# Fused attention, MLP and gate: the last 96 MLP features as extra columns of two projection units, exponentials kept in PSUM, and the additions of the products with V on GpSimd

## The chip, the cores and the metric

The kernel runs on one core of a Trainium2 chip. The metric is device time in microseconds (us), the median of several executions. In the text PE is TensorE, DVE is VectorE, ACT is ScalarE, POOL is GpSimd and SP is SyncE, which issues the DMAs.

## The reference

`x` is 2048 tokens of 512 numbers in fp32. Cut to what matters:

```python
xn = layernorm(x)
# A: sliding, dilated attention: 32 heads of 16, each token sees 8 tokens, 2 apart
q, k, v = split(xn @ wqkv)                     # 512 -> 3 * 512
logits = einsum("hsd,hswd->hsw", q, k[pos - 2*w]) * 16**-0.5   # w = 0..7, -1e9 where pos-2w < 0
s = einsum("hsw,hswd->hsd", softmax(logits), v[pos - 2*w]) @ wo
# B: MLP, F = 1376 features, and the gate
h = gelu(layernorm(xn) @ w1 + b1)              # 512 -> 1376 = 10 * 128 + 96
g = silu(h @ w2 + b2)                          # 1376 -> 512
out = x + s * g
```

## The kernel before

**Matmuls.** Every fp32 operand of a large matmul is written as a sum of two fp16 numbers (hi and lo), and three of the four cross products are computed, so 512 input features take 4 x 3 = 12 matmuls of 128x128 weights. Three kinds of work fill PE:

- *Projection units.* Tokens 0, 2, 4, ... and 1, 3, 5, ... are two residue classes `c`; with 4 blocks of 8 heads (`hb`) they give 8 units `u`. `qkv(c, hb, u)` computes one unit: 8 token tiles `i`, each 12 matmuls with 384 moving columns (128 each of q, k, v) into one PSUM tile, which ACT copies into `U[u % 2]` (L825). DMAs then copy the rows that neighbouring partitions need.
- *MLP.* The tokens are 4 chunks `ch` of 512; the 1376 features are 11 tiles `f`, the last of 96 (`FL`). `mlp1` (L1112) computes one feature tile of a chunk in 12 matmuls of 512 columns into a PSUM tile `mh`; ACT applies GELU there (L1129) and writes the fp16 hi part (L1133); DVE writes the lo part (L1137). For three early tiles PE subtracts hi in PSUM by a diagonal matrix `dg` instead (L1143) and ACT writes lo (L1146). `mlp2` (L1159) then takes the tile, two tiles later (`LAG`), in 4 x 3 matmuls of 512 columns into four accumulating PSUM tiles `z`. The 96-feature tile has its own buffer `hlast`, with a row of ones for the bias of the second layer, written by POOL (L1312).
- *Output projection.* L1026, from the transposed attention outputs `oT`.

**Attention of a unit** is elementwise, on DVE: 4 products q·k of 128x2048 (L873) each followed by a reduction (L877) into the logits `L` (128x512 in SBUF); maximum and subtraction (L908, L909); the exponential on ACT, in place (L912); sum, reciprocal and normalisation (L914 to L916); then 4 products with V, `pv(0)` to `pv(3)`, 128x2048 each (L946; L998 for the last unit), which have to be added up: 2048 + 2048 + 2048 down to 1024 numbers. DVE does some of these additions (L937). The rest, 128x1024 each, are put on POOL (L978) beside the next unit's reductions: `beside` puts a one-element copy from the next unit's product ahead of each (`gate`, L977), so that the addition starts once that product is done and runs while DVE reduces it. Then `emit_o` writes the output as hi (ACT, L925) and lo (DVE, L927), and a transposing DMA brings it into `oT`.

**Order.** `Plan` collects all operations with estimated durations, dependencies and priorities, and places them in the order of one simulated execution (with drawn disturbances, `SEEDS`). Each engine then runs its queue in that fixed order. Rings of buffers (`Ring`) are shared out in the same order. The PSUM has eight banks of 128x512 fp32: rings `ps` (2) and `mh` (2), and four `z`.

Of the kernel before, what the change touches and what calls it, by code (L numbers as in the profile page):

```python
# [19 lines left out]
P = 128  # L20
# [4 lines left out]
FL = F - (NF - 1) * P  # L25
NI = 8
# [8 lines left out]
W1C = [0, 2048, 4096, 5120, KT * F]  # L35
# [60 lines left out]
class Plan:  # L96
# [238 lines left out]
    def issue(self):  # L335
# [4 lines left out]
        for t, o in order:  # L340
# [4 lines left out]
SEEDS = ((500165, 389854, 427978, 647943, 394648, 289068, 629827, 866434, 58414, 290909, 969430, 478841,  # L345
          326988, 34468, 300308, 816254, 306888, 41293, 60788, 308971, 890734, 237800, 376148, 36800, 231455,
          772755, 355690, 761464),)
# [17 lines left out]
PS1 = 0.72  # L365

# [26 lines left out]
def tile_mixer(ctx, tc, a_x, a_wqkv, a_wo, b_w1, b_b1, b_w2, out):  # L393
# [47 lines left out]
    wq = sb.tile([P, NHB, 2, KT, 384], F16, name="wq")  # L441
    w1 = sb.tile([P, 2, KT, F], F16, name="w1")
# [7 lines left out]
    hlast = sb.tile([P, 2, 512], F16, name="hlast")  # L450
# [12 lines left out]
    R_ps = Ring(psum, [P, 512], F32, 2, "ps")  # L463
    R_mh = Ring(psum, [P, 512], F32, 2, "mh")
# [109 lines left out]
    def prep_q(hb):  # L574
        col = R_s.new()
        for k in range(0, KT, 2):
            def go(k=k):
                src = stq[hb]()[:, k * 384:(k + 2) * 384]
                nc.scalar.activation(wq[:, hb, 0, k:k + 2].bitcast(BF16),
                                     src.rearrange("p (k e) -> p k e", k=2), AF.Square,  # L580
                                     accum_out=col.t[:, k // 2:k // 2 + 1])
            act(768, go, [("stq", hb, k)] + ([("yf", 2)] if hb == 0 and k else []), [(col, k), ("wqh", hb, k), ("wqh", hb, k + 1)],
                aps=2, holds=stkey[hb])
# [194 lines left out]
    IORD, IORD0 = [2, 3, 1, 4, 5, 6, 7, 0], [2, 3, 0, 1, 4, 5, 6, 7]  # L778

    def qkv(c, hb, u):  # L780
# [13 lines left out]
        for n, i in enumerate(IORD if u else IORD0):  # L794
# [3 lines left out]
            b = (R_mh if more else R_ps).new()  # L798

            def mm(n0=0, n1=12, y=y, o=o, b=b):  # L800
                for n in range(n0, n1):
                    (s, t), k = ((0, 0), (1, 0), (0, 1))[n // KT], n % KT
                    nc.tensor.matmul(b.t[:, 0:384], y[:, s, k, o:o + P], wq[:, hb, t, k],  # L803
# [11 lines left out]
            for n0, n1 in zip([0] + ends, ends):  # L815
                pe(n1 - n0, 384, lambda mm=mm, n0=n0, n1=n1: mm(n0, n1), [("yh" if n1 <= 4 else "y", c, i)] +
                   [("wq" if n1 == 12 else "wqh", hb, k) for k in range(min(n1, KT))], [b],
                   after=pl.users([b]) | (left if n0 == 0 else set()), slack=QSLACK if u > 1 and n0 == 0 else 0.0)
            rw = [b, csk[i], ("kz", ub)], [("q", ub, i), ("k", ub, i), ("v", ub, i)]
            if i in on_dve:  # L820
# [6 lines left out]
                AF.Identity, scale=cs.t[:, cp(i):cp(i) + 1]), *rw, prio=PEV)  # L827

# [29 lines left out]
    def attention(c, hb, u):  # L858
# [9 lines left out]
        for n, g in enumerate(range(4)):  # L868
# [34 lines left out]
        def over_r(t):  # L903
# [8 lines left out]
        act(512, lambda: nc.scalar.activation(L.t, L.t, AF.Exp, scale=DH ** -0.5), Lk + [("warm",)], Lk, aps=0,  # L912
            table="exp", prio=PEV, hold=False)
        dve(512, lambda: nc.vector.tensor_reduce(sx.t, Lt(), AX.X, ALU.add), Lk, [sx], port=False)  # L914
        dve(64, lambda: nc.vector.reciprocal(sx.t, sx.t), [sx], [sx], f=6.0, port=False)
        dve(512, lambda: nc.vector.tensor_tensor(Lt(), Lt(), over_r(sx.t), op=ALU.mult),  # L916
            [sx] + Lk, Lk)
# [21 lines left out]
        if u < 7:  # L939
# [5 lines left out]
            def pv_to(g, dst, w):  # L945
                dve(2048, lambda: nc.vector.tensor_tensor(  # L946
                    dst().rearrange("p (r f d) -> p r f d", r=2, d=DH),
                    L3()[:, 2 * g:2 * g + 2].rearrange("p r (f o) -> p r f o", o=1)
                    .to_broadcast([P, 2, 64, DH]),
                    slots(Ut, VH, 2 * g).rearrange("p r (f d) -> p r f d", d=DH), op=ALU.mult),  # L950
                    Lk + vk + [("vh", ub, 0), ("vh", ub, 1), ("vh0", ub)], w)

            def addto(a, b):
                add(2048, lambda: a.t, lambda: b.t, lambda: a.t, [a, b], a)
            acc = pv(0)
            p1 = pv(1)
            if u in OWN:

                t2 = f32v(oT, 1)[:, 0, 2048:4096]
                pv_to(2, lambda: t2, [("p2",), ("oTst", 2)])  # L960
                addto(acc, p1)
                p3 = pv(3)
                add(1024, lambda: acc.t[:, 0:1024], lambda: t2[:, 0:1024], lambda: acc.t[:, 0:1024], [acc, ("p2",)], acc)
            else:
                p2 = pv(2)
                addto(acc, p1)
                p3 = pv(3)
                addto(acc, p2)
# [4 lines left out]
            def beside(x, y, upper=False):  # L973
                def go(pr, p=PR_U * (u + 1) + 500):
                    def fn():
                        d = x.t[:, 1024:2048] if upper else x.t[:, 0:1024]
                        nc.gpsimd.tensor_copy(gate, pr.t[0:1, 0:1])  # L977
                        nc.gpsimd.tensor_tensor(d, d, y(), op=ALU.add)  # L978
                    pool(2.45, fn, [acc, p3, pr] + [("p2",)] * (u in OWN), [x, ("gate",)], prio=p)
                return go  # L980
# [4 lines left out]
            if u in OWN:  # L985
                pend.append(beside(acc, lambda: t2[:, 1024:2048], True))
            pend.extend([beside(acc, lambda: acc.t[:, 1024:2048]),
                         beside(p3, lambda: p3.t[:, 1024:2048]),
                         beside(acc, lambda: p3.t[:, 0:1024]), rest])
        else:  # L990

            for h in range(2):
                m = []
                for g in range(2):
# [53 lines left out]
    def wo_last():  # L1048
        rings = [R_ps, R_ps, R_mh, R_mh] + R_z
# [50 lines left out]
    def w1_parts(k, f0, f1):  # L1100
        return [m for m in range(4) if W1C[m] < k * F + f1 and W1C[m + 1] > k * F + f0]

    def mlp1(ch, f):
        M = P if f < NF - 1 else FL
# [4 lines left out]
        def mm(n0, n1):  # L1109
            for n in range(n0, n1):  # L1110
                k, (s, t) = n // 3, ((0, 0), (0, 1), (1, 0))[n % 3]
                nc.tensor.matmul(b.t[0:M], w1[:, s, k, f * P:f * P + M], yT[ch][:, t, k],  # L1112
                                 start=(n == 0), stop=(n == 11))

        for n0 in range(0, 12, 3) if ch == 0 and f < 3 else (0,):
# [3 lines left out]
               [("w1", m) for k in range(n0 // 3, n1 // 3) for m in w1_parts(k, f * P, f * P + M)], [b],  # L1119
               after=pl.users([b]))  # L1120
        if f < NF - 1:
            h = R_h.new()
            hi, lo = (lambda: h.t[:, 0]), (lambda: h.t[:, 1])
        else:
            h = ("hlast",)
            hi, lo = (lambda: hlast[:, 0]), (lambda: hlast[:, 1])
        hk = (h, 0) if f < NF - 1 else ("hlast", 0)
        with prio(PR_H + pl.prio * 1e-6):
            act(512, lambda: nc.scalar.activation(  # L1129
                b.t[0:M], b.t[0:M], AF.Gelu_apprx_tanh, bias=b1T[0:M, f:f + 1],  # L1130
                scale=hsc[0:M, 1:2]), [b, ("b1T",), ("hsc",)], [b], aps=2, table="gelu")

            act(512, lambda: nc.scalar.activation(hi()[0:M], b.t[0:M], AF.Identity,  # L1133
                                                  scale=hsc[0:M, 2:3]),
                [b] + [("hseq", NF * ch + f - 1)] * (NF * ch + f > 0), [hk, ("hseq", NF * ch + f)])
            if NF * ch + f in DVE_LO:
                dve(512, lambda: nc.vector.scalar_tensor_tensor(  # L1137
                    lo()[0:M], b.t[0:M], hsc[0:M, 2:3], hi()[0:M], op0=ALU.mult,
                    op1=ALU.subtract), [b, hk], [h], port=False, c=0.14)
                hq[f] = (hi, lo, M if f < NF - 1 else M + 1, h, hk)  # L1140
                return

# [323 lines left out]
```

## Time and profile before

| what | value |
|---|---|
| three executions | 412.53, 413.24, 413.51 us; median 413.24 |
| span of the profiled execution | 411.5 us (the time of an execution is some 1.8 us more: 413.24 - 411.5) |
| PE busy | 406.5 us, 99% of the span, 2086 matmuls |
| DVE busy | 387.3 us, 94%, 372 instructions |
| ACT busy | 222.4 us, 54% |
| POOL busy | 114.8 us, 28% |
| DMA | 44.83 MB, mean 109 GB/s |

The profile holds one execution. Instructions of a line, operation and shape form a group with a count, a busy time and the mean of one in ns; busy times of matmuls include their pipelined ends, so the distance from one matmul's start to the next one's is read from the chain that ended last. Idle time in front of an instruction is put down to the engine or the DMA that released it.

### The profile page before, as it was taken

To read this page: it belongs to the slowest core of one execution; us is meant where nothing else is said; L and a number is where in the kernel's file an instruction comes from. 1 tells how busy PE (TensorE), PEld (TensorE's weight loads), DVE (VectorE), ACT (ScalarE), POOL (GpSimd) and SP (SyncE) were. 2 spreads that over 40 slices of the span, in tenths; PEclk is the share of its full clock that TensorE was granted. 3 is DMA by queue.
4 is the path that set the end of the run, shared out by engine and by line. 5 is a ranking of instruction groups with operands and counts; after the bars stand their busy time and mean duration, and the time that the engine had idled before them with its cause. 6 is when DMAs were issued, how large, how long until landed. Compare 5 with 4: busy or idle time off the path is not lost.

```text
span 411.5 us, 5549 instructions
## 1 busy us (share of the span) xinstructions
PE 406.5 (99%) x2086; PEld 206.7 (50%) x2086; DVE 387.3 (94%) x372; ACT 222.4 (54%) x357; POOL 114.8 (28%) x160
## 2 busy tenths in 40 slices
PE   8999999999999999999999999999999999999996
PEld 5565544446544554455444644445655554444443
DVE  4999999999999999999999989999989999999955
ACT  4999999976479377332673261127311582244500
POOL 6620442052822150015201500055037400340022
PEclk9999999999999999999999999999999999999999
DMA  8972350500343557600740070302063356008034
GB/s 289 414 268 86 89 205 2 204 2 1 91 99 132 63 159 170 83 0 2 178 165 2 0 165 29 104 0 74 4 205 115 102 181 165 0 2 256 2 78 177
DMA packets 42666, 44.83 MB, mean 109 GB/s; under 512 B 27496, under 2 KB 27936, under 8 KB 42128
## 3 DMA queue, kind: packets, MB, share of 16 engines
q1 hardware_dynamic: 42640, 44.49, 36.8%
q8 instruction: 16, 0.26, 0.3%
q14 instruction: 10, 0.08, 0.1%
HBM read 23.53 MB, written 7.34 MB: 75 GB/s over the span
## 4 chain that ended last, share of the span: by engine, by line
PE 97%; DMA 1%; DVE 1%; SPq 0%; POOL 0%; issue 0%
PE z L1159 28%; PE ps L803 27%; PE mh L1112 26%; PE ps L1026 6%; PE mh L803 2%; PE z L1026 2%; PE mh L1026 1%; PE ps L1112 1%; DMA prod<-in_A_x_dram 1%; PE z L705 1%; PE mh L810 1%; DVE U L1082 0%; DVE U L1085 0%; DVE bn L662 0%; PE ps L810 0%; POOL lw L636 0%
## 5 line engine op out<-in xcount | busy, mean ns | idle before, releaser
L1112 PE MATMUL mh<-yT,w 128*128 128x512 f16 (+1 forms) x504 | 115.7, 379 | 0.0
L803 PE MATMUL ps<-wq,yT 128*128 128x384 f16 x684 | 115.0, 326 | 0.0
L1159 PE MATMUL z<-w,h 128*128 128x512 f16 x480 | 110.8, 379 | 0.0
L803 PEld LDWEIGHTS <-yT 128*128 128x128 f16 x744 | 72.3, 98 | 49.4 <-ACT yT L720 0.4
L1112 PEld LDWEIGHTS <-w 128*128 128x128 f16 (+1 forms) x528 | 52.8, 100 | 60.9
L1129 ACT ACTIVATE mh<-mh,b1T,hsc 128x512 f32<-128x512 f32 (+1 forms) x42 | 31.5, 750 | 87.1 <-PE mh L1112 87.0
L1159 PEld LDWEIGHTS <-h 128*128 128x128 f16 x480 | 46.8, 98 | 55.6
L873 DVE TENSOR_TENSOR prod<-U 128x2048 f32<-128x2048 f32 x32 | 72.9, 2282 | 1.3 <-DMA U<-U 0.9
L877 DVE TENSOR_REDUCE L<-prod 128x128 f32<-128x2048 f32 x32 | 73.1, 2285 | 0.8
L825 ACT ACTIVATE U<-ps,cs 128x384 f32<-128x384 f32 x56 | 32.4, 579 | 60.6 <-PE ps L803 59.1
L946 DVE TENSOR_TENSOR prod<-L,U 128x2048 f32<-128x2048 f32 x25 | 60.0, 2422 | 0.2
L977 POOL COPY gate<-prod 1x1 f32<-1x1 f32 x24 | 4.2, 175 | 156.6 <-DVE prod L873 156.6
L978 POOL TENSOR_TENSOR prod<-prod 128x1024 f32<-128x1024 f32 x14 | 32.8, 2346 | 0.0
L1026 PEld LDWEIGHTS <-oT 128*128 128x128 f16 x204 | 19.8, 98 | 21.7
L937 DVE TENSOR_TENSOR prod<-prod,prod 128x2048 f32<-128x2048 f32 x13 | 29.7, 2282 | 0.0
L1026 PE MATMUL ps<-wo,oT 128*128 128x512 f16 (+1 forms) x132 | 28.5, 367 | 0.0
L1133 ACT ACTIVATE h<-mh,hsc 128x512 f16<-128x512 f32 x38 | 26.0, 684 | 0.8
L1137 DVE SCALAR_TENSOR_TENSOR h<-mh,hsc,h 128x512 f16<-128x512 f32 x36 | 26.3, 731 | 0.1
L978 POOL TENSOR_TENSOR prod<-prod,oT 128x1024 f32<-128x1024 f32 x3 | 10.0, 3324 | 41.6 <-DVE prod L937 41.6
L1019 POOL TENSOR_TENSOR f<-f,f 128x512 f32<-128x512 f32 x4 | 10.6, 2655 | 21.9 <-DMA U<-U 18.2
L978 POOL TENSOR_TENSOR prod<-prod,prod 128x1024 f32<-128x1024 f32 x7 | 16.4, 2346 | 0.0
L1019 POOL TENSOR_TENSOR U<-U,f 128x512 f32<-128x512 f32 x4 | 5.5, 1380 | 34.9 <-DVE U L1091 34.9
(184 smaller groups left out, 406.4 us busy)
## 6 DMA issues: line engine op xcount, KB each, us to landing
f<-in_A_x_dram SPq DMA_DIRECT2D x31, 256.0 KB, 3.6
U<-U SPq DMA_DIRECT2D x16, 392.0 KB, 3.9
gd<-f SPq DMA_DIRECT2D x12, 256.0 KB, 3.5
oT<-in_B_w_dram SPq DMA_DIRECT2D x2, 1024.0 KB, 9.5
yT<-in_B_w_dram SPq DMA_DIRECT2D x2, 1024.0 KB
f<-gd SPq DMA_DIRECT2D x8, 256.0 KB, 3.4
out_dram<-f SPq DMA_DIRECT2D x8, 256.0 KB, 3.0
out_dram<-U SPq DMA_DIRECT2D x7, 256.0 KB, 2.0
```

What stands on the lines that cost most here:

```text
L803: nc.tensor.matmul(b.t[:, 0:384], y[:, s, k, o:o + P], wq[:, hb, t, k], start=(n == 0), stop=(n == 11))
L825: act(384, lambda i=i, b=b: nc.scalar.activation(U3[:, i:i + 31:15, :], b.t[:, 0:384].rearrange("p (t e) -> p t e", t=3), AF.Identity, sca ...
L873: first = dve(2048, lambda p2=p2, g=g: nc.vector.tensor_tensor(p2(), q, slots(Ut, KH, 2 * g), op=ALU.mult), qk + [("kh", ub, 0), ("kh", ub ...
L877: first.then = dve(2048, lambda pr=pr, g=g: nc.vector.tensor_reduce(L3()[:, 2 * g:2 * g + 2], pr.t.rearrange("p (r f d) -> p r f d", r=2, ...
L937: dve(n, lambda: nc.vector.tensor_tensor(d(), a(), b(), op=ALU.add), keys, [dkey])
L946: dve(2048, lambda: nc.vector.tensor_tensor(dst().rearrange("p (r f d) -> p r f d", r=2, d=DH), L3()[:, 2 * g:2 * g + 2].rearrange("p r (f ...
L978: nc.gpsimd.tensor_tensor(d, d, y(), op=ALU.add)
L1026: nc.tensor.matmul(b.t[:, cols], oT[:, hb, i // 4, s, i % 4], wo[:, t, hb, cols], start=(hb == 0 and n == 0), stop=(hb == last and n == 2))
L1112: nc.tensor.matmul(b.t[0:M], w1[:, s, k, f * P:f * P + M], yT[ch][:, t, k], start=(n == 0), stop=(n == 11))
L1129: act(512, lambda: nc.scalar.activation(b.t[0:M], b.t[0:M], AF.Gelu_apprx_tanh, bias=b1T[0:M, f:f + 1], scale=hsc[0:M, 1:2]), [b, ("b1T",) ...
L1137: dve(512, lambda: nc.vector.scalar_tensor_tensor(lo()[0:M], b.t[0:M], hsc[0:M, 2:3], hi()[0:M], op0=ALU.mult, op1=ALU.subtract), [b, hk], ...
L1159: nc.tensor.matmul(z.t, hl[s][0:K, t * P:(t + 1) * P], w2[0:K, w, f], start=(f == 0 and n == 0), stop=(f == NF - 1 and n == 2))
```

## The change

1. **The last 96 features in two projection units.** The units `u = 2` and `u = 6` (head block 2 of each residue class) get weights `wqr` of 384 + 96 columns: the last 96 columns of `w1` stand beside those of q, k and v. Their 16 token tiles take 480 moving columns a matmul. The `mlp1` of the 96-feature tile and `hlast` go. Since these features now come out with tokens on partitions, a new chain `rest1` handles a chunk: ACT copies 4 times 96 columns out of PSUM, POOL adds the bias, ACT does GELU and hi over 128x384, DVE lo, POOL writes the column of ones, and one transposing DMA writes `hlT`, from which `mlp2` of `f = 10` reads.
2. **No subtraction on PE.** The three L1143 matmuls, `dg` and the ACT lo parts go; DVE writes all lo parts.
3. **Exponentials in PSUM.** ACT writes the exponentials to a PSUM tile `E`, and the sum, the normalisation and the products with V read it there. `ps` and `mh` become one ring of 3 banks; `E` has 1.
4. **Additions on POOL.** For `u < 7` POOL does all additions of the products with V as seven of 128x1024: two right behind `pv(1)`, without a gate, and five gated, four on the next unit's products and one on its shifted logits. For the last unit POOL does the first addition of the first half. `emit_o` comes one step later than before.
5. The seeds of the plan differ, and with them, and with the new operations, the order on all engines. `PREST` sets when the last piece of the `w1` split is placed. One more small DMA loads the bias of the 96 features (`b1r`).

```diff
-    w1 = sb.tile([P, 2, KT, F], F16, name="w1")
+    wqr = sb.tile([P, 2, KT, 384 + FL], F16, name="wqr")
+    wqs = sb.tile([P, NHB - 1, 2, KT, 384], F16, name="wqs")
+    w1 = sb.tile([P, 2, KT, FM], F16, name="w1")
...
-    R_ps = Ring(psum, [P, 512], F32, 2, "ps")
-    R_mh = Ring(psum, [P, 512], F32, 2, "mh")
+    R_ps = R_mh = Ring(psum, [P, 512], F32, 3, "ps")
+    R_E = Ring(psum, [P, 512], F32, 1, "E")
...
+        rest = u in RESTU
+        ncol = 384 + FL * rest
...
-                    nc.tensor.matmul(b.t[:, 0:384], y[:, s, k, o:o + P], wq[:, hb, t, k],
+                    nc.tensor.matmul(b.t[:, 0:ncol], y[:, s, k, o:o + P], wqr[:, t, k] if rest else wq[hb][:, t, k],
...
+            if rest:
+                ch = 2 * c + i // 4
+                hp = hrest[ch] = hrest.get(ch) or R_f.new()
+                act(FL, lambda i=i, b=b, hp=hp: nc.scalar.activation(
+                    hp.t[:, i % 4 * FL:(i % 4 + 1) * FL], b.t[:, 384:384 + FL], AF.Identity, scale=hsc[:, 1:2]),
+                    [b, ("hsc",)], [(hp, i % 4)], prio=PEV)
...
-            if pend and (n or u - 1 in OWN):
-                pend.pop(0)(pr)
-                if n == 3:
-                    pend.pop(0)()
+            if pend:
+                pend.pop(0)(pr, [pr])
...
-        act(512, lambda: nc.scalar.activation(L.t, L.t, AF.Exp, scale=DH ** -0.5), ...
+        act(512, lambda: nc.scalar.activation(E.t, L.t, AF.Exp, scale=DH ** -0.5), ...
+        if pend:
+            pend.pop(0)(L, Lk)
+            pend.pop(0)()
...
-                    L3()[:, 2 * g:2 * g + 2].rearrange("p r (f o) -> p r f o", o=1)
+                    E3()[:, 2 * g:2 * g + 2].rearrange("p r (f o) -> p r f o", o=1)
...
+            def sums(x, s, y, keys):
+                pool(2.4, lambda: nc.gpsimd.tensor_tensor(x.t[:, s], x.t[:, s], y(), op=ALU.add), [x] + keys, [x])
...
-                addto(acc, p1)
-                p3 = pv(3)
-                addto(acc, p2)
+            for s in (lower, upper):
+                sums(acc, s, lambda s=s: p1.t[:, s], [p1])
...
+            pend.extend([beside(acc, upper, lambda: t2[:, upper], [pk]),
+                         beside(acc, lower, lambda: t2[:, lower], [pk]),
+                         beside(p3, lower, lambda: p3.t[:, upper], []),
+                         beside(acc, lower, lambda: acc.t[:, upper], []),
+                         beside(acc, lower, lambda: p3.t[:, lower], [p3]), rest])
...
+    def rest1(ch):
+        hp, h16 = hrest.pop(ch), R_f.new()
...
+        pool(..., lambda: nc.gpsimd.tensor_tensor(t3(), t3(), b1r..., op=ALU.add), ...)
+        pool(0.4, lambda: nc.gpsimd.memset(h4()[:, :, :, FL:P], 0.0), hk, [(h16, 2)], port=False)
+        pool(0.25, lambda: nc.gpsimd.tensor_scalar(h4()[:, :, 0, FL:FL + 1], ...
+        act(4 * FL, lambda: nc.scalar.activation(hp.t[:, 0:4 * FL], hp.t[:, 0:4 * FL], AF.Gelu_apprx_tanh),
+            hk, hk, aps=0, table="gelu")
+        act(4 * FL, lambda: nc.scalar.activation(h4()[:, :, 0, 0:FL], t3(), AF.Identity, scale=hsc[:, 2:3]), ...
+        dve(4 * FL, lambda: nc.vector.scalar_tensor_tensor(
+            h4()[:, :, 1, 0:FL], t3(), hsc[:, 2:3], h4()[:, :, 0, 0:FL], op0=ALU.mult, op1=ALU.subtract), ...
+        dma(P * 2048, lambda: nc.sync.dma_start_transpose(
+            hlT.rearrange("p t a k -> p (t a) k"), h16.t.bitcast(F16)), ...
...
-            pe(1, 512, lambda: nc.tensor.matmul(b.t[0:M], dg[0:M, 0:M], hi()[0:M], start=False,
-                                                stop=True, skip_group_check=True), ...
-            act(512, lambda: nc.scalar.activation(lo()[0:M], b.t[0:M], AF.Identity, ...
```

In the changed kernel's line numbers the projection stands on L807, `mlp1` on L1153 and `mlp2` on L1185; q·k product and reduction are L883 and L887, the products with V L960, the sum, reciprocal and normalisation of the exponentials L928 to L930, the lo parts of the MLP L1173 and of the outputs L941; the ungated additions are L970, the gate and the gated additions L987 and L988; `rest1` runs from L1122 to L1136.

Two places show how the queues differ. The first is DVE where the MLP starts, from the last pieces of the weight splits (L551, L552) to the lo parts of the first three feature tiles (`h` with three buffer numbers). In the kernel before:

```order
L551 SCALAR_TENSOR_TENSOR w_77<-h_104,hsc,w_77 128x384
L877 TENSOR_REDUCE L_101<-prod_91 128x2x64
L551 SCALAR_TENSOR_TENSOR w_78<-yT_82,zsc,w_78 128x1024 x2
L1137 SCALAR_TENSOR_TENSOR h_105<-mh_159,hsc,h_105 128x512
L877 TENSOR_REDUCE L_101<-prod_92 128x2x64
L1137 SCALAR_TENSOR_TENSOR h_106<-mh_160,hsc,h_106 128x512
L551 SCALAR_TENSOR_TENSOR w_78<-yT_83,zsc,w_78 128x1024
L1137 SCALAR_TENSOR_TENSOR h_104<-ps_157,hsc,h_104 128x512
```

And now, DVE at the same place:

```order
L552 SCALAR_TENSOR_TENSOR wqr<-h_106,hsc,wqr 128x4x96
L552 SCALAR_TENSOR_TENSOR w_79<-yT_84,zsc,w_79 128x1024
L1173 SCALAR_TENSOR_TENSOR h_107<-ps_159,hsc,h_107 128x512
L883 TENSOR_TENSOR prod_94<-U_85 128x2048
L887 TENSOR_REDUCE L_103<-prod_94 128x2x64
L1173 SCALAR_TENSOR_TENSOR h_108<-ps_160,hsc,h_108 128x512
L1173 SCALAR_TENSOR_TENSOR h_106<-ps_161,hsc,h_106 128x512
```

Ahead of the second lo part there now stand a whole product and its reduction, where one reduction stood; the PSUM tiles read are the three of the shared ring.

The second place is POOL between the attention of the first unit and that of the second. Before, the last gated addition of the first unit, and the first of the second:

```order
L977 COPY gate<-prod_92 1x1
L978 TENSOR_TENSOR prod_93<-prod_93,prod_91 128x1024
L650 TENSOR_TENSOR lw_150<-lw_150,halves 128x8
L977 COPY gate<-prod_91 1x1
L978 TENSOR_TENSOR prod_92<-prod_92,oT 128x1024
```

And now, from the fourth gated addition of the first unit to the two ungated ones of the second (`b1r` and the two lines after the fifth addition belong to `rest1`):

```order
L987 COPY gate<-prod_94 1x1
L988 TENSOR_TENSOR prod_95<-prod_95 128x1024
L651 TENSOR_TENSOR lw_152<-lw_152,halves 128x8
L1122 TENSOR_TENSOR f_96<-f_96,b1r 128x384
L987 COPY gate<-L_104 1x1
L988 TENSOR_TENSOR prod_95<-prod_95,prod_93 128x1024
L1125 MEMSET f_98 128x8x32
L1126 TENSOR_SCALAR f_98<-f_98,hsc 128x4
L970 TENSOR_TENSOR prod_94<-prod_94,prod_93 128x1024 x2
```

The last addition of a unit now waits for the next unit's logits, and two additions with no gate follow. DVE, across the same place, has the second unit's products with V; before:

```order
L946 TENSOR_TENSOR prod_92<-L_102,U_85 128x2048
L946 TENSOR_TENSOR prod_93<-L_102,U_85 128x2048
L1137 SCALAR_TENSOR_TENSOR h_104<-mh_159,hsc,h_104 128x512
L946 TENSOR_TENSOR oT<-L_102,U_85 128x2048
L937 TENSOR_TENSOR prod_92<-prod_92,prod_93 128x2048
```

and now:

```order
L960 TENSOR_TENSOR prod_93<-E_162,U_86 128x2048
L941 SCALAR_TENSOR_TENSOR o_105<-prod_95,osc,o_105 128x2x512
L1173 SCALAR_TENSOR_TENSOR h_106<-ps_160,hsc,h_106 128x512
L960 TENSOR_TENSOR prod_95<-E_162,U_86 128x2048
L883 TENSOR_TENSOR prod_93<-U_85 128x2048
L1173 SCALAR_TENSOR_TENSOR h_107<-ps_159,hsc,h_107 128x512
```

The additions L937 are gone from DVE, and the next unit's first product with K (L883) stands between the products with V.

More of the change, by code (lines that the diff above doesn't have):

```diff
@@ L449, in tile_mixer @@
     b1T = sb.tile([P, NF], F32, name="b1T")
-    hlast = sb.tile([P, 2, 512], F16, name="hlast")
+    hlT = sb.tile([P, 4, 2, P], F16, name="hlT")
+    b1r = sb.tile([P, FL], F32, name="b1r")
     gd = dr.tile([DIL, NI, P, D], F32, name="gd")
@@ L797, in qkv @@
             o = (i % 4) * P
-            b = (R_mh if more else R_ps).new()
+            b = (R_E if u == 0 and n == 0 else R_mh if more else R_ps).new()
             def mm(n0=0, n1=12, y=y, o=o, b=b):
@@ L1118, in mlp1 @@
                [("y", c, 4 * j + i) for i in range(4)] +
[L1119 removed]
+               [("w1", m) for k in range(n0 // 3, n1 // 3) for m in w1_parts(k, f * P, f * P + P)], [b],
                after=pl.users([b]))
[L1121 to L1126, printed above, removed]
```

173 lines of the change are left out of this document (90 added, 83 removed).

## The prediction

> **What bounds the kernel.** I read the busy times first, then the chain that ended last, then how far apart matmuls start, and last the waits.
>
> ```profile
> PE 406.5 (99%) x2086; PEld 206.7 (50%) x2086; DVE 387.3 (94%) x372; ACT 222.4 (54%) x357; POOL 114.8 (28%) x160
> PE 97%; DMA 1%; DVE 1%; SPq 0%; POOL 0%; issue 0%
> ```
>
> The first line has busy time and share of the span, the second the shares of the chain. PE and DVE are both nearly full, so the shares alone don't say which one sets the end; the chain says PE. Pieces of that chain follow: start, duration, what.
>
> ```profile
> 51.79 2.59 PE z L1159 x12
> ...
> 91.36 15.60 PE ps L803 x96
> ...
> 109.55 2.59 PE z L1159 x12
> ...
> 399.31 7.47 PE z L1026 x39
> ```
>
> 96 matmuls of 384 columns take 15.60 us, 162.5 ns each. 12 of 512 columns take 2.59 us, 215.8 ns each, early and late alike. From 28 us to the last matmul each piece of the chain is a count times one of these two numbers and starts where the one ahead ends: PE has no idle time there that less DVE work could fill. The waits agree; those of PE, in all:
>
> ```profile
> PE z L1265 <- PEq L1437: 0.8, 1, 0.8
> PE z L705 <- DVE f L698: 0.2, 1, 0.2
> PE z L739 <- DVE f L731: 0.2, 1, 0.2
> ```
>
> The Trainium skill, Perfetto Trace Analysis, Identifying the Most-Contended Engine, says that matmul busy time is a poor measure of how near TensorE is to its limit, and that weight loads are a better one; here they are 50%. By that rule DVE at 94% would be the engine to relieve. The trace disagrees: the pitch, not the busy time, shows the queue without a gap. What the rule would make of the time is the last rival.
>
> **The change on PE.** Removed are the 96-feature tiles and the three diagonal products.
>
> ```profile
> L1112 PE MATMUL mh<-yT,w 128*96 128x512 f16 x48 | 11.0, 379 | 0.0
> L1143 PE MATMUL mh<-h,dg 128*128 128x512 f16 x2 | 0.8, 378 | 0.0
> L1143 PE MATMUL ps<-h,dg 128*128 128x512 f16 x1 | 0.4, 376 | 0.0
> L803 PE MATMUL ps<-wq,yT 128*128 128x384 f16 x684 | 115.0, 326 | 0.0
> ```
>
> The means (379) include pipelined ends; on the path counts the pitch, 215.8. So 48 x 0.2158 = 10.36 us and 3 x 0.2158 = 0.65 us go. Added are 96 columns to 2 units x 8 tiles x 12 = 192 matmuls. The trace has no 480 columns; the pitch lies between 162.5 and 215.8 ns, so the addition is between 0 and 192 x 53.3 = 10.2 us, and the net between -11.0 and -0.8 us. I take the straight line: 53.3/128 = 0.416 ns a column, 96 columns 40 ns, 192 x 40 = 7.68 us, since both points lie on nearly one line through the origin. Net: 7.68 - 10.36 - 0.65 = -3.33 us. `mlp2` keeps its count.
>
> **DVE.** Rows by shape, with count, busy time and mean:
>
> ```profile
> L946 DVE TENSOR_TENSOR prod<-L,U 128x2048 f32<-128x2048 f32 x25 | 60.0, 2422 | 0.2
> L937 DVE TENSOR_TENSOR prod<-prod,prod 128x2048 f32<-128x2048 f32 x13 | 29.7, 2282 | 0.0
> L1137 DVE SCALAR_TENSOR_TENSOR h<-mh,hsc,h 128x512 f16<-128x512 f32 x36 | 26.3, 731 | 0.1
> L998 DVE TENSOR_TENSOR prod<-L,U 128x2048 f32<-128x2048 f32 x4 | 9.1, 2284 | 0.0
> L916 DVE TENSOR_TENSOR L<-L,mx 128x512 f32<-128x512 f32 x8 | 5.5, 684 | 0.1
> L937 DVE TENSOR_TENSOR prod<-prod,oT 128x1024 f32<-128x1024 f32 x3 | 5.1, 1712 | 0.0
> L721 DVE TENSOR_TENSOR yT<-z,yT 128x512 f16<-128x512 f32 x6 | 4.0, 682 | 0.0
> L1137 DVE SCALAR_TENSOR_TENSOR hlast<-mh,hsc,hlast 96x512 f16<-96x512 f32 x4 | 2.9, 736 | 0.1
> L1304 DVE TENSOR_SCALAR dg<-ident,hsc 128x128 bf16<-128x128 f32 x1 | 0.7, 651 | 0.0
> L551 DVE SCALAR_TENSOR_TENSOR w<-h,hsc,w 128x384 f16<-128x384 f32 x1 | 0.6, 606 | 0.0
> ```
>
> Twelve of the 13 large additions go, 12 x 2.282 = 27.4 us; the three smaller ones, 5.1; `hlast`'s lo parts, 2.9; `dg`, 0.7. Three lo parts come, 2.2, and four of 128x384 in `rest1`, 4 x 0.606 = 2.4. That is -31.5 us. The products with V read the exponentials from PSUM, each number 16 times over; no row shows that. A 512-column operation takes 682 ns with one input in PSUM and 684 with none, so I take 2.28 us (L998); that also ends the 25 x 0.14 = 3.5 us by which L946 exceeds L998, which the next rows explain. DVE comes to about 352 us. Lower end: this saving; upper end: an access that halves the rate, 32 x 2.28 = 73 us more.
>
> ```profile
> 129.12 2.37 POOL L978 TENSOR_TENSOR prod<-prod,oT 128x1024 f32<-128x1024 f32 x1 [12.85 <-DVE prod L937]
> 129.62 4.01 DVE L946 TENSOR_TENSOR prod<-L,U 128x2048 f32<-128x2048 f32 x1
> ...
> 83.98 5.26 POOL L978 TENSOR_TENSOR prod<-prod,oT 128x1024 f32<-128x1024 f32 x1 [14.12 <-DVE prod L937]
> 86.96 0.74 DVE L1137 SCALAR_TENSOR_TENSOR h<-mh,hsc,h 128x512 f16<-128x512 f32 x1
> ```
>
> A product with two SBUF inputs beside a POOL addition takes 4.01 us instead of 2.28; an operation with an input in PSUM beside one keeps its 0.74. So the two ungated additions should run beside products from `E` free of charge. They do free the buffer of `pv(1)` 2 x 2.35 = 4.7 us late: where DVE has only L941, L1173 and one product ahead of the next L883 into that buffer, about 4.3 us, L883 waits some tenths, and up to 2 us where L941 is slowed. Over seven units this is under 14 us, against idle DVE time of about 408 - 352 = 56 us (24 before). It costs nothing on PE as long as DVE is ahead.
>
> **POOL and `rest1`.**
>
> ```profile
> L978 POOL TENSOR_TENSOR prod<-prod 128x1024 f32<-128x1024 f32 x14 | 32.8, 2346 | 0.0
> L1019 POOL TENSOR_TENSOR f<-f,f 128x512 f32<-128x512 f32 x4 | 10.6, 2655 | 21.9 <-DMA U<-U 18.2 <-DVE f L1040 3.6
> L636 POOL TENSOR_TENSOR lw<-lw,halves 128x8 f32<-128x8 f32 x1 | 3.5, 3466 | 0.0
> L1312 POOL TENSOR_SCALAR hlast<-hlast,hsc 1x512 f16<-1x512 f16 x1 | 2.5, 2536 | 17.4 <-DVE hsc L525 17.4
> yT<-f SPq DMA_TRANSPOSE x8, 3.8
> L825 ACT ACTIVATE U<-ps,cs 128x384 f32<-128x384 f32 x56 | 32.4, 579 | 60.6 <-PE ps L803 59.1
> L1129 ACT ACTIVATE mh<-mh,b1T,hsc 128x512 f32<-128x512 f32 x38 | 28.5, 751 | 72.0 <-PE mh L1112 71.9
> ```
>
> POOL's additions go from 24 to 7 x 7 + 2 = 51, 27 x 2.35 = 63 us more; with four bias additions (at most 2.7 each) it is busy some 190 of 408 us. An addition of 2048 costs 2 x 2.35 us there against 2.28 on DVE. The Trainium skill, GPSIMD Engine Reference, Engine selection, speaks against this part: elementwise additions belong on VectorE, GpSimd being about twice as slow with two inputs. The trace agrees, 4.69 against 2.28. On work this is a loss of 63 - 33 us; it is free since POOL was 72% idle, unless its lateness reaches PE (third rival).
>
> ACT gets 16 copies of 96 columns, each below L825's 579 ns, against a tile of 12 x 202.5 = 2430 ns on PE: 1.16 us of ACT a tile, hidden. `rest1` for the first chunk is bounded by this gate, the second unit's third:
>
> ```profile
> 104.30 0.17 POOL L977 COPY gate<-prod 1x1 f32<-1x1 f32 x1 [4.68 <-DVE prod L873]
> ```
>
> Adding up DVE's new queue puts it near 106. Behind it POOL has an addition (2.35), the bias (1.0 scaled down from 2346 ns for 1024 columns, 2.66 at most), the masks and zeros (about 1), L636 (3.5) and the ones (L1312 took 2.5 for 512 numbers of a partition; for 4, under 0.5): 114.4 to 116. Landing 3.8 later, `hlT` is there at 118.2 to 119.8; GELU, hi and lo run beside L636. PE wants it at about 120.3: the projection unit starts some 4.3 us later in the queue than at 91.36, at 95.7, takes 8 x 2.43 = 19.4, then two groups of 2.59 stand ahead. Slack 0.5 to 2 us; in the other chunks more.
>
> **The start of the MLP** is where I find the least slack. DVE before:
>
> ```profile
> 39.17 2.34 DVE L551 SCALAR_TENSOR_TENSOR w<-oT,hsc,w 128x2048 f16<-128x2048 f32 x1
> ...
> 42.31 1.27 DVE L551 SCALAR_TENSOR_TENSOR w<-o,hsc,w 128x1024 f16<-128x1024 f32 x1
> ...
> 46.87 2.46 DVE L551 SCALAR_TENSOR_TENSOR w<-yT,zsc,w 128x1024 f16<-128x1024 f32 x2
> 49.26 0.74 DVE L1137 SCALAR_TENSOR_TENSOR h<-mh,hsc,h 128x512 f16<-128x512 f32 x1
> ...
> 52.77 2.14 DVE L551 SCALAR_TENSOR_TENSOR w<-yT,zsc,w 128x1024 f16<-128x1024 f32 x1
> ```
>
> Before, the first lo part ends at 50.0 and PE uses it at 51.79. In the new order the reduction trades places with the 2048-column split, which now starts at about 42.3; behind it stand 2.3 + 1.2 + 2.4 + 0.6 us of splits, another one of 1.2 to 2.1 (the second, beside POOL), and the lo part, 0.7: it ends at 50.7 to 51.6. PE has the same work ahead and wants it at 51.7. The second lo part stands behind a product and a reduction, 2 x 2.28 + 0.73 = 5.3 us later; PE uses it 2 x 2.59 = 5.2 later. So both are just in time. With three shared banks the fourth feature tile waits for the same lo part. I put the cost at 0, the cover being a slack of 0.1 to 1.0 us.
>
> **Sum.** The profiled span of 411.5 becomes 411.5 - 3.33 = 408.1; it stands 1.8 below the median of the runs. The time is 413.24 - 3.33 = 409.9. Its own range, with 0.4 us either way for the 480-column pitch (2 ns on 192) and up to 0.6 of early stalls: 409.2 to 410.9.
>
> **Rivals.**
>
> 1. *DVE late at the start.* One operation of 2.28 us more ahead of the first lo part than I count makes PE wait 2.28 less the slack, 1.3 to 2.2 us: 411.2 to 412.1, say 411.6. For it: the slack above, and the next lo parts up to 71 us hang on the same queue. Against: all of them are one lateness, paid once. Chance 0.14.
> 2. *Products from PSUM slow.* If each of the 32 costs 1.1 us more than 2.28, DVE is as full as before (35/32); at 1.7 (56/32) its idle time is used up and the end moves with it. At double duration DVE has 352 + 73 = 425 us, with before's 24 idle 449 us: slower. For it: no row shows such a read. Against: 682 against 684 ns. Chance 0.06.
> 3. *POOL's chain late.* `hlT` or a unit's output comes late by more than its slack, since POOL's five gated additions hang on the next unit's products and the small L636 takes 3.5 us in the same queue. One more addition (2.35) and an L636 (3.5) ahead in one or two chunks, less the slack: 2 to 4 us, 411.9 to 413.9, say 412.5, no measurable change. Chance 0.14.
> 4. *Not the expected bound.* If DVE's queue set the end, its relief of 35 us would bring the time down to 413 - 35 = 378 at the least. For it: 94% busy. Against: a pitch of 215.8 ns without gaps. Chance 0.02. (By the rule of Perfetto Trace Analysis this would be the likely case; the trace does not agree.) If 480 columns cost what 512 do, net -0.8 us: 412.4; the straight line speaks against it. Chance 0.02.
>
> **How the numbers follow.** The forecast, 409.9, has 0.62. A change of 0.3% (1.24 us) is about what a measurement of this kernel can tell from none, so faster means below 412.0. Faster: 0.62, 0.11 of the first rival, 0.04 of the third, 0.02 of the fourth: 0.79. Same: 0.03 + 0.08 + 0.02 = 0.13. Slower: 0.06 + 0.02 = 0.08. The range 409.2 to 412.4 leaves out the second rival, the worse half of the third and what falls below, about 2 in 10.
>
> **What would show it.** Right: the 480-column group x192 with pieces of 12 in 2.43 us; PE near 99% with no wait above 1 us after 28 us; DVE near 352 us busy, waiting for POOL or ACT; products with V at 2.28; 51 POOL additions of 2.35. Wrong: PE waiting for DVE between 51 and 71 us (first rival), for `hlT` or ACT's copies (third), or L960 far above 2.28 (second).

## The result and the profile after

The changed kernel took 410.0 us (median of 4 runs, 409.62 to 410.8) beside 412.95 for the kernel before on the same chip: ratio 0.9935, 95% interval 0.9919 to 0.995. Forecast was 409.9, with 409.2 to 412.4. The span of the profiled execution is 407.9 us (forecast 408.1).

The page's busy times, and the shares of the chain that ended last:

```profile
PE 403.2 (99%) x2035; PEld 200.5 (49%) x2035; DVE 365.5 (90%) x359; ACT 225.4 (55%) x373; POOL 181.3 (44%) x207
PE 97%; DVE 1%; DMA 1%; POOL 0%; issue 0%
```

PE's share is what it was; DVE has 22 us less to do, POOL 67 more. Pieces of the chain (start, duration, what) at the first of the two widened units and behind it:

```profile
95.69 19.44 PE ps L807 x96
115.14 2.59 PE z L1185 x12
117.72 2.59 PE ps L1153 x12
120.31 2.59 PE z L1185 x12
```

96 matmuls of 480 columns take 19.44 us, 202.5 ns each, the value taken from the straight line, and the unit starts at the 95.7 that the order gave. PE's waits, in all:

```profile
PE z L1293 <- PEq L1460: 0.8, 1, 0.8
```

That one is at the very start; the view lists no other wait of PE.

### The profile page after: what moved, and what is told of

Its sections match the earlier page's. It is cut to its first block, busy times and chain, and to the rows that moved or that the text cites. A ratio compares the mean times of both kernels' runs of the same rounds, so it can differ in the third digit from the quotient of the medians.

```text
span 407.9 us, 5562 instructions
## 1 busy us (share of the span) xinstructions
PE 403.2 (99%) x2035; PEld 200.5 (49%) x2035; DVE 365.5 (90%) x359; ACT 225.4 (55%) x373; POOL 181.3 (44%) x207
## 4 chain that ended last, share of the span: by engine, by line
PE 97%; DVE 1%; DMA 1%; POOL 0%; issue 0%
PE ps L807 32%; PE z L1185 28%; PE ps L1153 25%; PE ps L1040 7%; PE z L1040 2%; PE z L706 1%; PE ps L814 1%; DMA prod<-in_A_x_dram 1%; PE E L814 1%; PE E L1040 1%; PE z L740 0%; DVE U L1096 0%; DVE U L1099 0%; DVE bn L663 0%; POOL lw L637 0%
## 5 line engine op out<-in xcount | busy, mean ns | idle before, releaser
L1185 PE MATMUL z<-w,h 128*128 128x512 f16 x480 | 109.9, 379 | 0.0
L1153 PE MATMUL ps<-yT,w 128*128 128x512 f16 x480 | 109.8, 379 | 0.0
L807 PEld LDWEIGHTS <-yT 128*128 128x128 f16 x744 | 72.2, 98 | 56.6 <-ACT yT L721 0.4
L807 PE MATMUL ps<-wqs,yT 128*128 128x384 f16 x552 | 91.9, 326 | 0.0
L883 DVE TENSOR_TENSOR prod<-U 128x2048 f32<-128x2048 f32 x32 | 74.1, 2314 | 2.8 <-DMA U<-U 2.1
L1153 PEld LDWEIGHTS <-w 128*128 128x128 f16 x480 | 46.9, 98 | 56.5
L1185 PEld LDWEIGHTS <-h 128*128 128x128 f16 x480 | 46.6, 98 | 56.0
L887 DVE TENSOR_REDUCE L<-prod 128x128 f32<-128x2048 f32 x32 | 73.1, 2286 | 0.9
L1167 ACT ACTIVATE ps<-ps,b1T,hsc 128x512 f32<-128x512 f32 x40 | 29.9, 749 | 61.0 <-PE ps L1153 60.3
L970 POOL TENSOR_TENSOR prod<-prod,prod 128x1024 f32<-128x1024 f32 x14 | 35.1, 2529 | 52.2 <-DVE prod L960 52.2
L960 DVE TENSOR_TENSOR prod<-E,U 128x2048 f32<-128x2048 f32 x21 | 47.6, 2282 | 1.2 <-POOL prod L970 0.9
L987 POOL COPY gate<-prod 1x1 f32<-1x1 f32 x28 | 5.3, 190 | 77.3 <-DVE prod L883 77.3
L807 PE MATMUL ps<-wqr,yT 128*128 128x480 f16 x192 | 39.2, 366 | 0.0
L988 POOL TENSOR_TENSOR prod<-prod 128x1024 f32<-128x1024 f32 x14 | 32.8, 2345 | 0.0
L1173 DVE SCALAR_TENSOR_TENSOR h<-ps,hsc,h 128x512 f16<-128x512 f32 x40 | 29.7, 744 | 3.0 <-ACT h L1171 2.8
L1171 ACT ACTIVATE h<-ps,hsc 128x512 f16<-128x512 f32 x40 | 27.3, 682 | 0.6
L988 POOL TENSOR_TENSOR prod<-prod,yT 128x1024 f32<-128x1024 f32 x8 | 18.8, 2347 | 0.0
L941 DVE SCALAR_TENSOR_TENSOR o<-prod,osc,o 128x1024 f16<-128x1024 f32 (+1 forms) x9 | 15.9, 1768 | 2.7 <-ACT o L939 2.7
```

The costliest lines, as they stand in the source:

```text
L807: nc.tensor.matmul(b.t[:, 0:ncol], y[:, s, k, o:o + P], wqr[:, t, k] if rest else wq[hb][:, t, k], start=(n == 0), stop=(n == 11))
L883: first = dve(2048, lambda p2=p2, g=g: nc.vector.tensor_tensor(p2(), q, slots(Ut, KH, 2 * g), op=ALU.mult), qk + [("kh", ub, 0), ("kh", ub ...
L887: first.then = dve(2048, lambda pr=pr, g=g: nc.vector.tensor_reduce(L3()[:, 2 * g:2 * g + 2], pr.t.rearrange("p (r f d) -> p r f d", r=2, ...
L960: dve(2048, lambda: nc.vector.tensor_tensor(dst().rearrange("p (r f d) -> p r f d", r=2, d=DH), E3()[:, 2 * g:2 * g + 2].rearrange("p r (f ...
L970: pool(2.4, lambda: nc.gpsimd.tensor_tensor(x.t[:, s], x.t[:, s], y(), op=ALU.add), [x] + keys, [x])
L988: nc.gpsimd.tensor_tensor(x.t[:, s], x.t[:, s], y(), op=ALU.add)
```

## Experiments

Each kernel ran beside the kernel before. The first asks the question that the prediction left out: what the 96 features bring alone.

**E1, points 1 and 2 alone.** From the changed kernel:

```diff
-    R_ps = R_mh = Ring(psum, [P, 512], F32, 3, "ps")
-    R_E = Ring(psum, [P, 512], F32, 1, "E")
+    R_ps = Ring(psum, [P, 512], F32, 2, "ps")
+    R_mh = Ring(psum, [P, 512], F32, 2, "mh")
     # and attention() as in the kernel before
```

> Only the move of the 96 features and the lo parts (points 1 and 2 of the change); exponentials in SBUF, additions as before, PSUM rings ps 2 and mh 2. Theory (the gain is PE's alone): PE's queue is that of the changed kernel, 3.33 us shorter than before, so about 409.9 us. Rival (the relief of DVE was needed): DVE comes to about 390 us busy in a span of 408, 18 us idle instead of 42, PE waits for it in places and at least half of the gain is lost, 411.5 us or more.

423.09 us, ratio 1.025 (1.0237 to 1.0263): the rival's side, and slower than before, which neither expected. PE's waits, without those at the start:

```profile
PE ps L1038 <- DMA oT<-o: 4.2, 2, 3.6
PE mh L1151 <- DVE h L1171: 3.5, 1, 3.5
```

PE waits for a lo part on DVE, which frees a PSUM tile, and, at the end, for the last unit's output. DVE was busy 394.9 us. These waits are 7.7 of the 13.7 us by which this span, 421.6 us, exceeds that of the changed kernel; the last section shows what came behind one of them.

**E2, points 3 and 4 alone.** From the kernel before: `attention` of the changed kernel, and its rings.

> Only the exponentials in PSUM, the three shared banks and the additions on POOL (points 3 and 4); the 96 features keep their own tiles and the three diagonal products stay. Theory: PE's queue is that of before, so 412.6 to 413.5 us, no change, though DVE has some 20 us less to do. Rival (DVE's relief is worth time by itself): below 411.7 us. Rival on the other side (the shared banks cost something): PE waits after 28 us, above 414 us.

412.35 us, ratio 0.9992 (0.9984 to 1.0001): no change.

```profile
PE 405.9 (99%) x2086; PEld 206.8 (50%) x2086; DVE 360.5 (88%) x357; ACT 222.4 (54%) x358; POOL 178.1 (43%) x198
```

27 us less on DVE are worth nothing while PE has the same queue. The fourth rival, by which DVE's relief is time, falls; the three shared banks cost nothing.

**E3, 384 columns, and E4, 512 columns**, in the two widened units. `wqx` is `wqr` without its inner dimensions, with 32 columns more; a matmul of 512 columns reads 32 of the next block, which nobody uses.

```diff
-                    nc.tensor.matmul(b.t[:, 0:ncol], y[:, s, k, o:o + P], wqr[:, t, k] if rest else wq[hb][:, t, k],
+                    nc.tensor.matmul(b.t[:, 0:384], y[:, s, k, o:o + P], wq[hb][:, t, k],              # E3
+                    nc.tensor.matmul(b.t[:, 0:512 if rest else 384], y[:, s, k, o:o + P],              # E4
+                                     wqx[:, (t * KT + k) * 480:(t * KT + k) * 480 + 512] if rest else wq[hb][:, t, k],
```

> The changed kernel, but the 192 matmuls of the two units take 384 columns instead of 480 (the 96 features are left out; ACT copies 96 of the 384 columns in their place), the order of all queues being the same. Theory: each matmul costs 40 ns less and PE sets the end throughout, so 7.68 us go: 402.3 us, span 400.2. Rival (other engines are close behind): PE waits in places, less than half of it goes, 406 us or more.

> The changed kernel, but the 192 matmuls take 512 columns, 32 of them unused. Theory: 13.3 ns each, 2.56 us more on PE, all on the path: 412.6 us. Rival: the pitch of 480 columns is already that of 512, or PE has room, so 410.0 us.

E4: 411.87 us, ratio 0.9983 (0.9974 to 0.9991), so 0.48 points above the changed kernel's 0.9935, 2.0 us. Its chain has the pieces

```profile
95.27 20.72 PE ps L809 x96
...
267.04 20.72 PE ps L809 x96
```

20.72 - 19.44 = 1.28 us each, 2.56 together, as expected; its first 20 us were 0.4 us shorter than in the changed kernel's profile, a stretch in which the chain runs through the first load of `x`. By the two intervals the 2.0 us are good to about 0.7. E3: 404.57 us, ratio 0.9816 (0.9791 to 0.9841): 1.19 points below 0.9935, 4.9 of 7.68 us. Neither theory: PE sets most of the end, but with 7.7 us less on it waits appear:

```profile
PE ps L807 <- DVE f L1054: 3.1, 1, 3.1
PE z L1185 <- DMA hlT<-f: 1.0, 1, 1.0
```

The others are that close behind PE: `hlT`, wanted some microseconds sooner, is late, and a PSUM bank of the output projection is freed late by DVE. The profiled execution was the slowest of the six, 408.13 us, and had 3.4 us at half clock behind the wait of 3.1 us, so these waits name the places and are not the 2.8 us that the median lost.

**E5, E1 in another order.** E1 drew its order with seeds found for other work, so it may have been a poor one.

```diff
-SEEDS = ((663796, 176219, 842312, ...),)
+SEEDS = ((997180, 998266, 522521, 244921),)
```

> The kernel of the first experiment (points 1 and 2 alone) with other seeds, the best of some 2500 orders by the plan's own estimate. Theory (without its relief DVE cannot keep up with the shorter queue of PE): DVE stays near 390 us busy, PE still waits for it, and the time stays above 412.0 us, 413 to 418. Rival (the first experiment only drew a poor order): 409.6 to 411.

416.92 us, ratio 1.0115 (1.0087 to 1.0143), 6 us better than E1 and still slower than before. DVE 389.6 us busy. So order explains part of E1; this order, the one that was run, still loses. Not all of it is DVE's shortage: PE waits 1.8 us for a lo part on DVE, but also 2.3 us in the first 8 us, for the layer norm of the first tokens, with half clock behind it.

**E6, points 1 to 3, additions on DVE.** E5 with `E` in PSUM, three banks, and an order sought in the same way.

> Points 1 to 3 without point 4: the exponentials are read from PSUM, the additions stay on DVE as before, and the order is the best of some 2400 by the plan's estimate. Theory (the additions are the relief that counts): DVE near 390 us busy, 412 to 416 us. Rival (reading from PSUM is the relief that counts): 409.6 to 411.

413.06 us, ratio 1.0009 (0.9999 to 1.0018). DVE is 383.7 us busy, and the chain that ended last leaves PE in the last unit:

```profile
379.42 6.69 DVE prod L1012 x3
386.11 2.21 DVE prod L951
...
389.56 2.20 DVE prod L1012
...
392.28 2.28 DVE prod L951
394.56 0.66 DVE o L941
...
395.25 3.04 DMA oT<-o
```

The last unit's products and additions follow one another on DVE and its transposed output comes after PE wants it. So in this order the additions' move is needed too. Up to the last unit PE found its work in time here; whether it would be enough to move that unit's one addition alone was not tried.

**E7, the exponentials in SBUF**, in place, as before, all else as changed.

```diff
-        E = R_E.new()
+        E = L
```

> The changed kernel without point 3: the exponentials stay in SBUF, in place in the logits, and the products with V have two SBUF inputs; POOL does all additions. Theory (PSUM spares the products beside POOL's ungated additions): 14 products take about 4.0 us instead of 2.28, DVE comes to about 390 us, and PE waits: 411.5 to 415 us. Rival (where the exponentials stand does not matter): products at 2.3 us, 409.6 to 410.4.

428.61 us, ratio 1.0404 (1.0377 to 1.043). The mechanism is the expected one, the price several times as large. First the additions on POOL and a product beside them in this kernel, then in the changed one:

```profile
127.53 7.67 POOL L970 TENSOR_TENSOR prod<-prod,prod 128x1024 f32<-128x1024 f32 x2
129.22 3.77 DVE L960 TENSOR_TENSOR prod<-L,U 128x2048 f32<-128x2048 f32 x1
```

```profile
175.83 4.67 POOL L970 TENSOR_TENSOR prod<-prod,prod 128x1024 f32<-128x1024 f32 x2 [10.26 <-DVE prod L960]
176.26 2.28 DVE L960 TENSOR_TENSOR oT<-E,U 128x2048 f32<-128x2048 f32 x1
```

With two SBUF inputs each slows the other: two additions 7.67 us instead of 4.67, the product 3.77 instead of 2.28. The Trainium skill, SBUF — State Buffer, Who interferes with whom, has it that DVE with two SBUF inputs and GpSimd take turns at one pair of ports; the traces agree. DVE comes to 388.7 us, as expected, but POOL's delay returns to DVE, which waits for POOL's additions (6 us, L960 and L883), and PE waits in seven places.

**E8, 16 us more on DVE.**

```diff
+TWICE = (3,)
...
-                dve(2048, lambda: nc.vector.tensor_tensor(
+                m = 2 if g in TWICE else 1
+                dve(2048 * m, lambda: [nc.vector.tensor_tensor(
...
+                    ... op=ALU.mult) for _ in range(m)],
```

> The changed kernel with the fourth product with V of each of the first seven units computed twice, 7 x 2.28 = 16 us more on DVE, the plan knowing of it. Theory (DVE has room): DVE near 381 us busy, 27 us idle, a little more than before the change: 410.0 to 411 us. Rival (DVE is already on the path): each added us counts, up to 426 us.

422.52 us, ratio 1.0236 (1.0218 to 1.0254): 12.5 us for 16. It looks as if DVE had no room at all. PE waits above all in one place, for the last unit's output, and the clock was at half for 6.8 us from 389.8 on, within that wait and behind it:

```profile
PE ps L1043 <- DMA oT<-o: 7.4, 1, 7.4
```

**E9 and E10, more DVE work, reordered.** E8 with other seeds, and `TWICE = (2, 3)`, 32 us, with its own. 

> The kernel of the eighth experiment (16 us more on DVE) with other seeds, the best of some 2200 orders by the plan's estimate. Theory (DVE has room for 16 us, the first order used it badly): 409.8 to 411.5 us. Rival (DVE's idle time is waits that no order fills): 416 to 423.

> The changed kernel with two of the four products with V of the first seven units computed twice, 14 x 2.28 = 32 us more on DVE, and the best of some 3300 orders. By the prediction (the time rises only when 54 us are added): DVE near 396 us busy, 410 to 412 us. Rival (of DVE's 42 idle us some 25 to 30 cannot be used, as in the kernel before, which had 24): 415 to 421 us.

E9: 409.23 us, ratio 0.9917 (0.9902 to 0.9931): the 16 us are free, E8 was its order. E10: 416.98 us, ratio 1.0104 (1.0087 to 1.0121): 7 us of the 32 reach the end. So some 32 - 7 = 25 us of products fit, not 54; this is an estimate from one order. DVE's busy time rose by 24.0 us only, to 389.5, because in this order the outputs' lo parts take 8.9 us instead of 14.4; counted in busy time, the room is 24 - 7 = 17 us. Busy times by stage show where it lay. In the changed kernel (start:end us, length; then PE, PEld and DVE busy, each with its count):

```profile
120.00:240.00 120.00, 120.00 (x629) 61.25 (x628) 108.25 (x77) 70.34 (x102) 53.31 (x54) 1.00 0.43 103
240.00:360.00 120.00, 120.00 (x588) 57.14 (x587) 115.05 (x83) 47.32 (x72) 64.28 (x64) 1.00 0.36 96
360.00:400.00 40.00, 40.00 (x187) 18.11 (x186) 30.11 (x30) 12.87 (x18) 12.29 (x7) 1.00 0.39 112
```

and in E9:

```profile
120.00:240.00 120.00, 120.00 (x629) 61.34 (x628) 115.62 (x80) 66.82 (x98) 53.94 (x52) 1.00 0.38 92
240.00:360.00 120.00, 120.00 (x587) 57.18 (x586) 116.13 (x82) 46.81 (x71) 62.66 (x62) 1.00 0.34 96
360.00:400.00 40.00, 40.00 (x187) 18.11 (x185) 34.80 (x34) 13.87 (x18) 15.17 (x10) 1.00 0.37 106
```

DVE's 11.8 idle us between 120 and 240 shrink to 4.4 and the 9.9 between 360 and 400 to 5.2; between 240 and 360 4 to 5 stay in both. (These two kernels differ in order too; E12 below, with E9's order and no doubled products, idles 11.0, 8.3 and 7.2 us in the three stretches.) E10 keeps 3.7, 3.9 and 4.2 in the same stretches, and there PE waits.

**E11, E7 reordered**, the plan told of the shared port.

> The kernel of the seventh experiment (exponentials in SBUF, all additions on POOL), with the plan told that the products with V then share the port with POOL, and the best of some 2200 orders. Theory (the additions on POOL need the exponentials in PSUM): products beside POOL still slow or POOL waiting, above 414 us. Rival (only the order was poor): 410 to 412 us.

423.67 us, ratio 1.0275 (1.024 to 1.031). In neither of the two orders that were run do the additions on POOL pay with the exponentials in SBUF.

**E12, E9's queues without the doubled products.**

```diff
-                    ... op=ALU.mult) for _ in range(m)],
+                    ... op=ALU.mult) for _ in range(1)],
```

> The queues of the ninth experiment without the doubled products: 16 us less on DVE, all orders the same. Theory (PE's queue sets the end, DVE's 16 us lay in its idle time): the same time as the ninth, 409.0 to 409.7 us. Rival (DVE still holds PE up somewhere): below 408.6 us.

409.18 us, ratio 0.9919 (0.9906 to 0.9933), E9's time. With PE's queue full, 16 us on or off DVE change nothing. It is not told apart from the changed kernel, whose interval (0.9919 to 0.995) it touches: no better version was found.

Four kernels with points 1 and 2, each run in one order sought for it (the last is the change as it stands). The median of the kernel before lay between 412.5 and 413.0 us beside them; since E8 and E9 are 13 us apart by order alone, a difference of 3 us here can hold some of it:

| additions | exponentials in SBUF | in PSUM |
|---|---|---|
| on DVE | 416.92 (E5) | 413.06 (E6) |
| on POOL | 423.67 (E11) | 410.0 (the change) |

## Why the prediction was right, and where it was not

- *The sum on PE.* Right in its terms: the 480-column pieces take the 19.44 us forecast, so 10.36 + 0.65 - 7.68 = 3.33 us go; the span fell by 3.6, of which 0.2 lie in the first 25 us. E2 (the same queue, the same time), E4 (2.56 us more on PE) and E12 show that PE's queue set the end. Beside the kernel before the gain was 2.7 us (2.1 to 3.3, from the ratio), and 3.4 in E9 and E12, which have the same work on PE. That 409.9 met 410.0 to a tenth is in part luck: the base taken, 413.24, was 0.3 above the median of the kernel before in the same comparison, 412.95, and the gain between the medians, 2.95, 0.4 below the sum.
- *The rule that it set against the trace.* Of the two measures for TensorE in the section that it names, the Trainium skill, Perfetto Trace Analysis, Identifying the Most-Contended Engine, it used the weight loads and left out the other, the arithmetic done as a share of the peak. So what the trace disagrees with is half of that rule.
- *The work was not apportioned.* The prediction put the whole gain on PE's shorter queue and gave the relief of DVE no worth of its own. True of the whole, wrong of the parts: alone the features made the kernel slower (E1, E5). DVE then needs 389.6 us (E5); in the 408 of PE's new queue 18 would stay idle, fewer than in any kernel here that kept PE busy (before 24, E9 26). Points 3 and 4, worth nothing alone (E2), are the condition of the gain in the orders that were run.
- *DVE's sum.* 352 us forecast, 365.5 measured, the one term of the prediction that was clearly mis-sized; it cost nothing, since DVE stayed ahead of PE. The products from `E` came to the value taken:

```profile
L960 DVE TENSOR_TENSOR prod<-E,U 128x2048 f32<-128x2048 f32 x21 | 47.6, 2282 | 1.2 <-POOL prod L970 0.9
L941 DVE SCALAR_TENSOR_TENSOR o<-prod,osc,o 128x1024 f16<-128x1024 f32 x7 | 14.4, 2059 | 1.9 <-ACT o L939 1.9
L1133 DVE SCALAR_TENSOR_TENSOR f<-f,hsc,f 128x384 f16<-128x384 f32 x4 | 5.5, 1369 | 0.7 <-ACT f L1131 0.7
L883 DVE TENSOR_TENSOR prod<-U 128x2048 f32<-128x2048 f32 x32 | 74.1, 2314 | 2.8 <-DMA U<-U 2.1
```

  What was mis-sized are operations with two SBUF inputs that now stand beside work on POOL: the outputs' lo parts 2059 ns instead of 1278 (7 x 0.78 = 5.5 us; the four slow ones, of 1.6 to 3.1 us, lie beside POOL's ungated additions L970 and L1017), those of `rest1` 1369 instead of the 606 taken (3.1; the two slow ones, of 3.2 and 1.1 us, lie beside POOL), and a single product with K, 3.21 us beside POOL's split of weights at the start of the MLP (0.9). That is 9.5 us: the durations of all DVE operations together fell by 25.5 us, not by 35. The other 4 us are no work. The records of neighbouring operations on DVE overlap by some hundredths of a us each, 20.6 us in all before and 16.9 now, and the busy time counts such time once. The prediction named L941's slowing as a wait, and left it out of the sum. Of its up to 14 us of waiting for the buffer of `pv(1)` the products with K show none; one product with V waited 0.9 us for an addition.
- *The second rival's point.* "At 1.7 its idle time is used up" took all 56 idle us as room. E10 puts the point at 17 to 25 us, 0.5 to 0.8 a product. What holds the rest of the idle time was not separated; in E10 only 12 of DVE's 26 idle us lie between 120 and 400 us, the others mostly at the two ends of the kernel.
- *The first chunk's `rest1`.* The landing came inside the forecast, 118.2 to 119.8, by another path than the one forecast, so by luck.

```profile
106.34 3.14 POOL L1122 TENSOR_TENSOR f<-f,b1r 128x384 f32<-128x384 f32 x1
110.10 1.67 POOL L637 TENSOR_TENSOR lw<-lw,halves 128x8 f32<-128x8 f32 x1
111.73 3.16 DVE L1133 SCALAR_TENSOR_TENSOR f<-f,hsc,f 128x384 f16<-128x384 f32 x1 [0.66 <-ACT f L1131]
114.95 2.12 SPq L1136 DMA_TRANSPOSE hlT<-f  x1
```

  The gate came at 103.84 instead of 106, and POOL was done at 112.1, ahead of the 114.4 to 116 forecast. What held the DMA until 114.95 was the lo part on DVE, which the forecast had hidden beside L636: 3.16 us, beside a POOL addition, instead of 0.6. With a median of 4.3 us to landing `hlT` was there at 119.3, some 0.6 us ahead of the first weight load from it at 119.9. Nor are the prices of POOL's steps fixed. In the kernel before, L636 (now L637) stood beside a product with K:

```profile
106.80 2.28 DVE L873 TENSOR_TENSOR prod<-U 128x2048 f32<-128x2048 f32 x1
107.14 3.47 POOL L636 TENSOR_TENSOR lw<-lw,halves 128x8 f32<-128x8 f32 x1
```

  Now it stands behind that product (L883, from 106.34 to 108.62) and takes 1.67, while the bias stands beside it and takes 3.14 us, 1.0 in the other three chunks.
- *The start of the MLP.* The second lo part was just in time, the first less tight than forecast, since the 2048-column split began at 41.1 instead of 42.3:

```profile
48.92 0.75 DVE L1173 SCALAR_TENSOR_TENSOR h<-ps,hsc,h 128x512 f16<-128x512 f32 x1
49.59 3.21 DVE L883 TENSOR_TENSOR prod<-U 128x2048 f32<-128x2048 f32 x1
52.84 2.29 DVE L887 TENSOR_REDUCE L<-prod 128x128 f32<-128x2048 f32 x1
55.04 1.40 DVE L1173 SCALAR_TENSOR_TENSOR h<-ps,hsc,h 128x512 f16<-128x512 f32 x2
```

  The first ends at 49.7 (50.7 to 51.6 forecast), 1.9 us ahead of its use, the second at 55.7, 1 us ahead.

## What to carry to other kernels

Where two engines are nearly full, a change that shortens the queue of the one on the chain has to be priced against the room of the other, stage by stage; the idle time of the whole span overstates that room (42 us here, of which 17 to 25 could be used). A part that brings nothing by itself can be what makes another part pay, so ask of each part what the rest would do without it. When a queue's order is planned, an experiment that changes its operations needs an order of its own before it says anything: E8 lost 12.5 us and E9, with the same work, none.

## What the runs showed of the hardware

Behind some waits PE runs at half clock. E1, a wait of 3.5 us, then, after five matmuls at full pace up to 223.0, the next ones, and those behind them (the number ahead of the last two is the granted clock):

```profile
218.00:222.00 4.00, 0.54 (x4) 0.18 (x2) 4.00 (x4) 1.73 (x3) 0.00 (x0) 1.00 0.15 53
222.90:226.10 3.20, 3.20 (x10) 1.15 (x8) 3.20 (x2) 0.00 (x0) 0.00 (x0) 0.52 0.00 0
226.30:229.50 3.20, 3.20 (x16) 1.47 (x15) 2.42 (x3) 1.33 (x2) 0.00 (x0) 0.98 0.00 0
```

From 223.0 to 226.4, 3.4 us, the clock is 0.5: eight matmuls start 427 ns apart instead of 216, which adds 1.7 us to the wait. That is one reason why E1 lost more than its waits. Waits of 1 to 2 us, as in E10, showed nothing of the kind, but the length of the wait alone does not decide it. In E7 a wait of 3.06 us, from 318.9 to 322.0, had no half clock behind it, and one of 2.42 us, from 352.4 to 354.8, had:

```profile
317.26:320.67 3.41, 1.67 (x11) 0.88 (x9) 3.38 (x2) 0.58 (x1) 1.64 (x2) 1.00 0.10 37
320.67:324.09 3.42, 2.09 (x13) 1.26 (x13) 3.39 (x5) 0.00 (x0) 2.10 (x2) 1.00 0.00 0
351.39:354.81 3.42, 1.03 (x5) 0.29 (x3) 3.42 (x3) 1.44 (x2) 0.59 (x1) 1.00 1.11 283
354.81:358.22 3.41, 3.37 (x8) 1.19 (x9) 3.41 (x3) 0.00 (x0) 1.17 (x2) 0.50 1.00 318
```

The first number behind the length is PE's busy time. Within each trace the clock changes stand whole multiples of 3.41 us apart, and the stretches here are cut at these marks. PE was idle for 2.4 us of the third stretch, and the fourth ran at half; the longer wait fell across two stretches, 1.7 and 1.3 us idle, and the clock stayed. In all fourteen traces of this case, the ends of the kernels included, every stretch with 2.3 idle us or more had half clock behind it, and none with 2.0 or less; nothing between was seen. The Trainium skill, TensorE: Matmul & The Clock Gate, HAM oscillation — how this bites in real kernels, warns of gaps on PE above some 3.4 us. The runs agree in the length of the stretch; as a limit for the wait it is too high here.
